# A de-interleaving turn of one input block laid out so that each phase is one copy, and a new seed for the order search

## The chip, the core and the metric

The kernel runs on one core of a Trainium2 chip. The metric is the device time of one execution in microseconds; the median of three runs of the kernel before is 252.25 us (252.25 to 252.41). Five engines work side by side: TensorE (PE, with its weight loads as PEld) multiplies, VectorE (DVE), ScalarE (ACT) and GpSimd (POOL) do elementwise work, and SyncE (SP) issues nearly all transfers.

## The reference

Two strided one-dimensional convolutions, a projection and a joint network. T is 4000, D is 512, both kernels have 5 taps, and U is 8.

```python
xp = jnp.pad(x, ((0,0),(pad,pad),(0,0)))
for i in range(K):
    h = h + jnp.einsum("btc,cd->btd", xp[:, i:i+T, :], w1[i])
h = _gelu(h)[:, ::2, :]
...
f = _gelu(f)[:, ::2, :]          # the same with w2 on h
fe = jnp.einsum("btd,de->bte", f, w_f)
ge = jnp.einsum("bud,de->bue", g, w_g)
j = jnp.tanh(fe[:, :, None, :] + ge[:, None, :, :])
return jnp.einsum("btud,dv->btuv", j, w_o)
```

Only even times of each convolution are kept. An output at time 2t needs inputs 2t-2 to 2t+2, so taps 0, 2 and 4 read only even input times (the even phase), and taps 1 and 3 only odd ones (the odd phase).

## The kernel before, in words

**Stages.** The first 426 outputs of the first convolution of batch 0 are computed directly, five taps each, while the rest of the inputs is still arriving (`direct`, line 811). The rest of both convolutions goes through fast products on triples of outputs (`Triple`, `Unit`), for which DVE and ACT form sums of input planes and of weights. Then come the projection (`fe`, `FeSeven`) and the joint network, in which ACT makes the tanh, DVE and POOL form sums and PE runs seven products per 4 tiles (`Seven`, `Plain`), with the results evicted by ACT and DVE and stored by SP.

**The direct stage.** Its input lies in `eo[phase, k, column]`: two phases, four channel groups k, channels on partitions. It is filled in two parts. Input block 0 (`xr[0]`, 512 times) is turned by PE transposes and copied by `turn(pp)` (line 610), one phase at a time. Input block 1 (`xr[1]`, 384 times, three consecutive times r = 0, 1, 2 on each of 128 partitions p, so that the time is 3p + r) is turned by `turn3` (line 628). It multiplies each 128x128 piece by `perm`, a permutation which puts the even partitions into the first 64 columns and the odd ones into the last 64. Since 3p + r is even when p and r have the same parity, one phase takes the even-partition half of r = 0 and r = 2 and the odd-partition half of r = 1. `turn3` before the change puts r = 0, 2, 1 into PSUM banks 4, 5, 6, each as (k, half, 64). ACT then copies out of them in four pieces: for each phase one piece with two of the three r (128x512) and one with the third (128x256). Each piece reads runs of 64 adjacent places and writes every third place of `eo`.

The order in which these steps are written down is: even turn of block 0, tap 0 on the 254 columns that block 0 covers, odd turn, tap 4 on them, `turn3`, tap 2 on them, then taps 0, 4, 2 on the remaining 172 columns (48 matmuls), and then taps 1 and 3 on all 426 columns (32 matmuls). Every tap is 4 output groups of 4 matmuls, accumulating in banks 0 to 3.

**What sets the order.** The program is a list of operations with the tiles that they read and write. `Plan.schedule` orders them per engine: `once` walks through a model of the engines with costs that are written down (for ACT 0.833 ns an element plus 0.05 us out of PSUM), taking on PE, SP and POOL the ready operation that was written first, on ACT and DVE the ready one with the earliest due time `late`. Evictions marked as flexible go to the engine that comes free. `learn` changes due times and puts holds on operations where the model has a gap on PE; `schedule` repeats that 600 times and keeps whatever does not make the modelled end later. The first six kinds of change are fixed ones, later ones are drawn from a random generator with the seed [4, tried]. Each engine then runs its list in order and waits on semaphores.

**Other names used below.** `w_sb` are the raw weights, `w_x` and `w_t` sums of weights made by DVE and ACT, `xa` and `xp` transposed input planes brought in by DMA transposes, `row` and `sd` intermediates of the triples; `acc` is PSUM. Line 507 is every matmul of `mm`, line 499 every ACT operation of `act`, line 494 every DVE operation of `tt`, line 654 the DVE multiply-add of `stt`, line 637 the matmul of `turn3`.

Of the kernel before, what the change touches and what calls it, by code (L numbers as in the profile page):

```python
# [7 lines left out]
ACT = mybir.ActivationFunctionType  # L8
ALU = mybir.AluOpType
BF16 = mybir.dt.bfloat16  # L10
FP16 = mybir.dt.float16
FP32 = mybir.dt.float32
P = 128
# [55 lines left out]
class Plan:  # L69
# [1 line left out]

    COMPUTE = ("pe", "act", "dve", "pool")
    HOP = 0.16
    PASSES = 600

    def __init__(self, nc):
        self.nc = nc
# [82 lines left out]
    def schedule(self, pred):  # L160
# [17 lines left out]
        best, tried = self.once(pred, succ, late, hold), 0  # L178
        for _ in range(self.PASSES):
            new = list(late), list(hold)  # L180
# [14 lines left out]
    def learn(self, pred, got, late, hold, tried):  # L195


        _, order, start, end, ready, _ = got
        place = {i: (e, p) for e, o in order.items() for p, i in enumerate(o)}
        gaps, t = [], 0.0  # L200
        for i in order["pe"]:
            if start[i] - t > 0.05 and start[i] > 6.0:
                gaps.append(i)
            t = end[i]
        if not gaps:
            return False
        kind, which = divmod(tried, len(gaps) + 1)
        if kind >= 6:
            rng = np.random.default_rng([4, tried])
            t = start[gaps[int(rng.integers(len(gaps)))]]  # L210
            for e in ("act", "dve"):
                for j in order[e]:
                    if t - 10.0 < start[j] < t and rng.random() < 0.15:
                        late[j] += float(rng.normal())
            return True
        step, wait = ((0.1, True), (0.5, False), (0.0, True), (2.0, True), (0.3, False), (1.0, True))[kind % 6]
        first = list(late)
        for i in gaps if which == len(gaps) else gaps[which:which + 1]:
            j = i
            for _ in range(30):  # L220
                done = [(end[q] + (self.HOP if w else 0.0), q) for q, w in pred[j].items()]
                if not done:
                    break
                q = max(done)[1]
                if self.ops[q].dma:
                    break
                e, p = place[q]
                if e in ("act", "dve") and p and start[q] > ready[q] + 0.03:
                    b = order[e][p - 1]
                    if wait and start[b] < ready[q] - 0.02 and first[b] > first[q]:  # L230
                        hold[b] = max(hold[b], ready[q] - 0.01)
                    late[q] -= step
                j = q
        return True
# [134 lines left out]
def bass_standalone__seq2seq_rnn_t_joint__speech_kernel(  # L369
# [22 lines left out]
    NK = D // P  # L392
# [12 lines left out]
    NT = 512  # L405
# [4 lines left out]
    with ExitStack() as es:  # L410
        cur = [16512]

        def at(name, shape, dtype, offset=None):
            o = cur[0] if offset is None else offset
            b = Buf(nc, name, shape, dtype, o)
            if offset is None:
                cur[0] = (b.end + 31) // 32 * 32
            return b
# [13 lines left out]
        xr = [Buf(nc, f"xr{i}", [4, NK, P], BF16, h_off + 16384 + i * 4096) for i in range(NX)]  # L432
# [7 lines left out]
        geT = at("geT", [NK * BU], FP32)  # L440
        gT = at("gT", [NK, BU], BF16)
        zero = at("zero", [NT], BF16)
        ident, perm = at("ident", [P], BF16), at("perm", [P], BF16)
        warm = at("warm", [2], FP32)
        xe = at("xe", [NK, 16], BF16)
        assert cur[0] <= 229368, cur[0]
        eo = Buf(nc, "eo", [2, NK, EW], BF16, w2_sb.end - w2_sb.bytes)
# [33 lines left out]
        ps = Psum(es.enter_context(nc.psum_tensor("acc", [P, 8 * NT], FP32)))  # L481
        block = es.enter_context(nc.Block(no_gpsimd_drain=True))
        pl = Plan(nc)
# [13 lines left out]
        def act(o, i, func, scale=1.0, bias=None):  # L497
            rd = (i,) if bias is None else (i, bias)
            pl.op("act", lambda e: e.activation(o.ap, i.ap, func, scale=scale,  # L499
                                                bias=0.0 if bias is None else bias.ap), rd, (o,),  # L500
                  o.ap.free_size() * 0.833e-3 + (0.05 if i.psum else 0.105 if bias is None else 0.186))

        def mm(o, pairs, start, stop, check=True):
# [13 lines left out]
        pl.op("pool", lambda e: e.affine_select(  # L517
            out=idv.ap, in_=zero[0:P].ap, compare_op=ALU.not_equal, fill=1.0, base=0,
            pattern=[[-1, P]], channel_multiplier=1), (zero[0:P],), (idv,))
        for i in range(2):  # L520
            pm = perm[i * P // 2:(i + 1) * P // 2]
            pl.op("pool", lambda e, pm=pm, i=i: e.affine_select(
                out=pm.ap, in_=zero[0:P // 2].ap, compare_op=ALU.not_equal, fill=1.0, base=-i,
                pattern=[[-2, P // 2]], channel_multiplier=1), (zero[0:P // 2],), (pm,))
        memset(eo[:, :, 15:16])
        memset(xa[:, :, 16 * -(-(NF + 2) // 16):16 * -(-(NF + 2) // 16) + 4])
# [5 lines left out]
        NR = (4, 3)  # L532
# [93 lines left out]
                    pl.op("dve", lambda e, o=o, v=v: e.tensor_copy(out=o.ap, in_=v.ap), (v,), (o,), vec_cost(o, (v,)))  # L626

        def turn3(cost):
            n, lo = NR[1], 16 + 2 * P
            place = [0, 2, 1]  # L630
            pv = [View(ps.h[:, (4 + i) * NT:(5 + i) * NT], np.array([4 + i]), True) for i in range(n)]
            for r in range(n):
                at_r = pv[place[r]]

                def fn(e, r=r, at_r=at_r):
                    for k in range(NK):
                        ins = e.matmul(at_r.ap[:, k * P:(k + 1) * P], lhsT=xr[1].h[:, r, k, :], rhs=perm.h[:, :],  # L637
                                       start=k == 0, stop=k == NK - 1, skip_group_check=True)
                    return ins
                pl.op("pe", fn, (xr[1][0:n], perm[:]), (at_r,), cost / n)  # L640

            def block(i0, i1, s0):
                ap = ps.h[:, (4 + i0) * NT:(4 + i1) * NT].rearrange("p (r k s c) -> p s k r c", r=i1 - i0, k=NK, s=2)
                return View(ap[:, s0], np.arange(4 + i0, 4 + i1), True)

            for pp in range(2):
                to = eo[pp, :, lo:lo + n * P // 2]
                for i0, i1, s0, o0 in ((0, 2, pp, pp), (2, 3, 1 - pp, 2 - 2 * pp)):
                    o = to.map(lambda a: a.rearrange("p k (c r) -> p k r c", r=n)[:, :, o0:o0 + i1 - i0, :])
                    act(o, block(i0, i1, s0), ACT.Copy)  # L650
                    pl.ops[-1].cost += 0.05

        def stt(eng, o, a, f, b):
            pl.op(eng, lambda e: e.scalar_tensor_tensor(  # L654
# [170 lines left out]
        turn(1, 0.43)  # L825
        direct(TAPS[1], 0, NH)
        turn3(0.67)
        direct(TAPS[2], 0, NH)
        for i in TAPS[:3]:
# [3 lines left out]
        for m in range(NK):  # L833
            v = ps.cols(m * NT, ND).map(lambda a: a.rearrange("p (q r) -> p r q", r=6))
# [447 lines left out]
        j = 2 + 4 * S1  # L1282
# [6 lines left out]
        fill = ["cc"] * 9 + ["c"] * 6 + ["p"] * 15  # L1289
# [4 lines left out]
        for i, q in enumerate(seven):  # L1294
            p = seven[i - 1] if i else None
            base = min([(p or q).jt] + plains[:1]) * P
            last = i + 1 == len(seven)
            r = []
# [60 lines left out]
```

## Time and profile before

| | |
|---|---|
| median of three runs | 252.25 us |
| the profiled execution | 252.33 us, its span 250.5 us |
| PE busy | 245.8 us (98%) |
| DVE, ACT busy | 210.1 us, 211.1 us (84% each) |
| POOL busy | 99.2 us (40%) |
| granted TensorE clock | 1.00 |

The time of an execution is the span of its instructions and some 1.8 us around it. Busy shares are averages: PE is the engine to look at, and what counts is where it stands still and who lets it go on.

### The profile page before, as it was taken

The page shows a single profiled execution, that of the slowest core. Times are in us where ns is not written, and L with a number is a line of the kernel's source. Part 1 is how long each engine was busy: PE and PEld are TensorE (multiplying, and loading weights), DVE is VectorE, ACT ScalarE, POOL GpSimd, SP SyncE. Part 2 cuts the span into 40 slices and gives each one's busy share as a digit, 9 for nine tenths or more (in the row PEclk, how much of TensorE's full clock was granted, in tenths as well). Part 3 has the DMA queues.
Part 4 walks back from the last instruction along what each step waited for, and adds up shares of the span by engine and source line. Part 5 has one row for each costly group of instructions (what it writes and reads, how often), then busy time and mean ns, then how long its engine had stood idle before and what let it go on. Part 6 is the DMA issues. An engine that isn't in the chain of part 4 may idle for free.

```text
span 250.5 us, 5277 instructions
## 1 busy us (share of the span) xinstructions
PE 245.8 (98%) x1948; PEld 183.3 (73%) x1948; DVE 210.1 (84%) x355; ACT 211.1 (84%) x351; POOL 99.2 (40%) x108
## 2 busy tenths in 40 slices
PE   8999999999999999999999999999999999999994
PEld 4777986666666666667556888777888878777883
DVE  2799998966999999398956889777999989986783
ACT  3399989859878767884599999999999999998772
POOL 2000000000000000000007978979799899888840
PEclk9999999999999999999999999999999999999999
DMA  6999999989000052000001043323345564555456
GB/s 224 322 213 188 168 187 168 188 162 352 7 3 0 0 166 89 0 4 0 0 3 42 0 147 109 125 86 111 120 152 167 167 190 154 165 177 183 150 191 207
DMA packets 54487, 31.86 MB, mean 127 GB/s; under 512 B 31518, under 2 KB 54206, under 8 KB 54462
## 3 DMA queue, kind: packets, MB, share of 16 engines
q1 hardware_dynamic: 54174, 31.37, 47.9%
q8 instruction: 15, 0.25, 0.4%
q10 hardware_dynamic: 288, 0.16, 0.2%
q14 instruction: 10, 0.08, 0.1%
HBM read 7.73 MB, written 16.38 MB: 96 GB/s over the span
## 4 chain that ended last, share of the span: by engine, by line
PE 97%; ACT 1%; ACTq 0%; issue 0%
PE acc L507 96%; ACT eo L499 1%; PE acc L618 1%; PE acc L637 0%; ACT og L1066 0%; ACTq L1092 0%; ACT ost L499 0%; ACTq L330 0%
## 5 line engine op out<-in xcount | busy, mean ns | idle before, releaser
L494 DVE TENSOR_TENSOR og<-acc,sn 128x512 bf16<-128x512 f32 x84 | 54.9, 682 | 7.9 <-PE acc L507 6.0
L499 ACT ACTIVATE jT<-feT,geT 128x1000 bf16<-128x1000 f32 (+5 forms) x60 | 57.5, 1017 | 0.3 <-DVE feT L494 0.3
L1146 POOL TENSOR_TENSOR ss<-jT 128x512 f16<-128x512 bf16 x33 | 38.5, 1175 | 41.3 <-DVE ss L1146 40.9
L507 PE MATMUL acc<-tw,ss 128*128 128x256 f16 x336 | 46.2, 273 | 0.0
L507 PE MATMUL acc<-row,w_sb 128*128 128x334 bf16 (+2 forms) x224 | 38.8, 296 | 0.0
L507 PEld LDWEIGHTS acc<-tw,ss 128*128 128x128 f16 x336 | 32.3, 98 | 7.6 <-ACT sn L1066 0.6
L507 PE MATMUL acc<-wo_sb,jT 128*128 128x256 bf16 (+1 forms) x208 | 33.3, 285 | 0.0
L1066 ACT ACTIVATE sn<-acc 128x512 f32<-128x512 f32 x48 | 29.7, 628 | 3.1 <-PE acc L507 2.3
L1067 DVE COPY sn<-acc 128x512 f32<-128x512 f32 x36 | 24.6, 685 | 7.0 <-PE acc L507 6.7
L507 PEld LDWEIGHTS acc<-row,w_sb 128*128 128x128 bf16 x224 | 21.1, 97 | 9.2 <-DVE acc L654 0.8
L491 POOL MEMSET hT<- 128x8 bf16 (+2 forms) x6 | 0.8, 148 | 61.8 <-ACT hT L499 45.0
L507 PEld LDWEIGHTS acc<-wo_sb,jT 128*128 128x128 bf16 x208 | 20.3, 98 | 5.0
L499 ACT ACTIVATE sd<-acc 128x334 f32<-128x334 f32 (+2 forms) x48 | 20.4, 432 | 3.4 <-PE acc L507 2.8
L1146 POOL TENSOR_TENSOR ss<-ss,jT 128x512 f16<-128x512 f16 x19 | 21.9, 1160 | 0.8 <-DVE ss L1146 0.8
L499 ACT ACTIVATE hT<-acc 128x334 bf16<-128x334 f32 (+3 forms) x36 | 15.5, 436 | 7.3 <-PE acc L507 6.7
L654 DVE SCALAR_TENSOR_TENSOR acc<-acc,sd 128x334 f32<-128x334 f32 (+2 forms) x24 | 11.6, 483 | 9.1 <-PE acc L507 9.0
L494 DVE TENSOR_TENSOR row<-row 128x1336 bf16<-128x1336 bf16 (+2 forms) x24 | 18.9, 796 | 0.0
L499 ACT ACTIVATE jX<-feT,geT 128x1000 bf16<-128x1000 f32 (+3 forms) x20 | 18.3, 963 | 0.0
L507 PE MATMUL acc<-xp,w_t 128*128 128x334 bf16 (+1 forms) x96 | 17.6, 305 | 0.0
L507 PE MATMUL acc<-hT,w_t 128*128 128x334 bf16 x96 | 17.5, 304 | 0.0
L507 PE MATMUL acc<-wo_sb,ss 128*128 128x256 bf16 x112 | 17.3, 273 | 0.0
L507 PE MATMUL acc<-xp,w_x 128*128 128x334 bf16 (+1 forms) x96 | 16.8, 305 | 0.0
(127 smaller groups left out, 496.7 us busy)
## 6 DMA issues: line engine op xcount, KB each, us to landing
out_dram<-og SPq DMA_DIRECT2D x42, 256.0 KB, 2.5
w_sb<-in_w_dram SPq DMA_DIRECT2D x10, 512.0 KB, 5.3
out_dram<-og SPq DMA_DIRECT2D x14, 128.0 KB, 2.1
out_dram<-ost SPq DMA_DIRECT2D x10, 128.0 KB, 1.9
xr<-in_x_dram SPq DMA_DIRECT2D x1, 512.0 KB, 3.4
wf_sb<-in_w_f_dram SPq DMA_DIRECT2D x1, 512.0 KB, 3.6
wg_sb<-in_w_g_dram SPq DMA_DIRECT2D x1, 512.0 KB, 4.7
wo_sb<-in_w_o_dram SPq DMA_DIRECT2D x1, 512.0 KB, 5.7
```

The source lines that it names most:

```text
L491: pl.op("pool", lambda e: e.memset(v.ap, 0.0), (), (v,))
L494: pl.op(eng, lambda e: e.tensor_tensor(out=o.ap, in0=a.ap, in1=b.ap, op=op), (a, b), (o,), 0.02 + 2.14e-3 * o.ap.free_size() if eng == "po ...
L499: pl.op("act", lambda e: e.activation(o.ap, i.ap, func, scale=scale, bias=0.0 if bias is None else bias.ap), rd, (o,), o.ap.free_size() * ...
L507: ins = e.matmul(o.ap, lhsT=l.ap, rhs=r.ap, start=start and n == 0, stop=stop and n == len(pairs) - 1, skip_group_check=not check)
L618: ins = e.transpose(pv.ap[:, r, k, :], xr[0].h[:, 2 * r + pp, 2 * h + k, :], ident.h[:, :])
L654: pl.op(eng, lambda e: e.scalar_tensor_tensor(out=o.ap, in0=a.ap, scalar=f, in1=b.ap, op0=ALU.mult, op1=add), (a, b), (o,), vec_cost(o, (a ...
L1066: pl.flex({"act": (lambda e: e.activation(o.ap, v.ap, ACT.Copy), 0.05 + n * 0.833e-3), "dve": (lambda e: e.tensor_copy(out=o.ap, in_=v.ap) ...
L1067: "dve": (lambda e: e.tensor_copy(out=o.ap, in_=v.ap), 0.065 + n * 1.04e-3)}, (v,), (o,))
L1146: fn = lambda e, o=S[i], x=x, y=y, op=op: e.tensor_tensor(out=o.ap, in0=x.ap, in1=y.ap, op=op)
```

## The change

Five edits. The permutation gets a third block of 64 columns that repeats the first, so that a slice of it also gives the order odd, even. `turn3` goes over k instead of r: for each k a bank holds six runs of 64 places, first the three of the even phase in the order of time, then the three of the odd phase; r = 1 writes the two middle runs together, r = 0 and r = 2 write one run in each half. It now uses banks 4 to 7. Each phase is then copied by one ACT operation over all four banks (128x768), even phase first; it reads every 64th place and writes adjacent places. The added 0.05 us in the planner's cost of these copies goes. The search takes 1200 rounds instead of 600, and another seed.

```diff
-    PASSES = 600
+    PASSES = 1200
...
-            rng = np.random.default_rng([4, tried])
+            rng = np.random.default_rng([13, tried])
...
-        ident, perm = at("ident", [P], BF16), at("perm", [P], BF16)
+        ident, perm = at("ident", [P], BF16), at("perm", [3 * P // 2], BF16)
...
-        for i in range(2):
+        for i in range(3):
             pm = perm[i * P // 2:(i + 1) * P // 2]
             pl.op("pool", lambda e, pm=pm, i=i: e.affine_select(
-                out=pm.ap, in_=zero[0:P // 2].ap, compare_op=ALU.not_equal, fill=1.0, base=-i,
+                out=pm.ap, in_=zero[0:P // 2].ap, compare_op=ALU.not_equal, fill=1.0, base=-(i % 2),
...
         def turn3(cost):
-            n, lo = NR[1], 16 + 2 * P
-            place = [0, 2, 1]
-            pv = [View(ps.h[:, (4 + i) * NT:(5 + i) * NT], np.array([4 + i]), True) for i in range(n)]
-            for r in range(n):
-                at_r = pv[place[r]]
-
-                def fn(e, r=r, at_r=at_r):
-                    for k in range(NK):
-                        ins = e.matmul(at_r.ap[:, k * P:(k + 1) * P], lhsT=xr[1].h[:, r, k, :], rhs=perm.h[:, :],
-                                       start=k == 0, stop=k == NK - 1, skip_group_check=True)
+            n, h, lo = NR[1], P // 2, 16 + 2 * P
+            for k in range(NK):
+                c0 = (4 + k) * NT
+                at_k = ps.cols(c0, 2 * n * h)
+
+                def fn(e, k=k, c0=c0):
+                    for r in range(n):
+                        if r % 2:
+                            o, pm = ps.h[:, c0 + 2 * h:c0 + 4 * h], perm.h[:, h:3 * h]
+                        else:
+                            o = ps.h[:, c0:c0 + NT].rearrange("p (s c) -> p s c", c=h)[:, r // 2:r // 2 + 5:4, :]
+                            pm = perm.h[:, 0:2 * h].rearrange("p (s c) -> p s c", s=2)
+                        ins = e.matmul(o, lhsT=xr[1].h[:, r, k, :], rhs=pm, start=r == 0, stop=r == n - 1,
+                                       skip_group_check=True)
                     return ins
...
             for pp in range(2):
-                to = eo[pp, :, lo:lo + n * P // 2]
-                for i0, i1, s0, o0 in ((0, 2, pp, pp), (2, 3, 1 - pp, 2 - 2 * pp)):
-                    o = to.map(lambda a: a.rearrange("p k (c r) -> p k r c", r=n)[:, :, o0:o0 + i1 - i0, :])
-                    act(o, block(i0, i1, s0), ACT.Copy)
-                    pl.ops[-1].cost += 0.05
+                v = ps.h[:, 4 * NT:8 * NT].rearrange("p (k j c) -> p k c j", k=NK, c=h)[:, :, :, n * pp:n * pp + n]
+                o = eo[pp, :, lo:lo + n * h].map(lambda a: a.rearrange("p k (c j) -> p k c j", j=n))
+                act(o, View(v, np.arange(4, 8), True), ACT.Copy)
```

More of the change, by code (lines that the diff above doesn't have):

```diff
@@ L628, in turn3 @@
         def turn3(cost):
-            n, lo = NR[1], 16 + 2 * P
-            place = [0, 2, 1]
-            pv = [View(ps.h[:, (4 + i) * NT:(5 + i) * NT], np.array([4 + i]), True) for i in range(n)]
-            for r in range(n):
-                at_r = pv[place[r]]
-                def fn(e, r=r, at_r=at_r):
-                    for k in range(NK):
-                        ins = e.matmul(at_r.ap[:, k * P:(k + 1) * P], lhsT=xr[1].h[:, r, k, :], rhs=perm.h[:, :],
-                                       start=k == 0, stop=k == NK - 1, skip_group_check=True)
-                    return ins
-                pl.op("pe", fn, (xr[1][0:n], perm[:]), (at_r,), cost / n)
@@ L642, in block @@
-            def block(i0, i1, s0):
-                ap = ps.h[:, (4 + i0) * NT:(4 + i1) * NT].rearrange("p (r k s c) -> p s k r c", r=i1 - i0, k=NK, s=2)
-                return View(ap[:, s0], np.arange(4 + i0, 4 + i1), True)
+            n, h, lo = NR[1], P // 2, 16 + 2 * P
[11 more added lines that the diff above has]
+                                       skip_group_check=True)
+                    return ins
+                pl.op("pe", fn, (xr[1][0:n], perm[:]), (at_k,), cost / NK)
```

## The prediction

> **What bounds the kernel now.** I read the page first, for the engine that is full:
>
> ```profile
> span 250.5 us, 5277 instructions
> PE 245.8 (98%) x1948; PEld 183.3 (73%) x1948; DVE 210.1 (84%) x355; ACT 211.1 (84%) x351; POOL 99.2 (40%) x108
> ```
>
> PE is busy for all but 4.7 us of 250.5. Then the chain of waits that ended last, in order of time, for what lies between PE's stretches:
>
> ```profile
> 5.89 3.84 PE acc L507 x32
> 9.73 0.68 PE acc L637 x12
> ...
> 10.44 2.33 ACT eo L499 x3
> ...
> 12.82 233.37 PE acc L507 x1852
> ```
>
> It leaves PE once before the end: after `turn3`'s matmuls (L637) it runs through three ACT copies into `eo`, 2.33 us, and then never leaves PE until 12.82 + 233.37 = 246.19. The waits of PE and of its weight loads, the second list after 12.9 us only, say the same:
>
> ```profile
> PE acc L507 <- PEq L1344: 0.8, 1, 0.8
> PE acc L507 <- ACT eo L499: 0.7, 1, 0.7
> ...
> PEld acc L507 <- DVE acc L654: 0.8, 3, 0.3
> PEld acc L507 <- ACT sn L1066: 0.6, 3, 0.3
> ...
> PEld acc L507 <- DVE xp L494: 0.2, 1, 0.2
> ```
>
> The matmuls have one wait inside the kernel, for `eo`. What the loads wait later (six such rows, from 0.8 down to 0.2, 2.6 us in all) is nearly all covered by matmuls still running, since PE shows no idle time of its own there. Now PE and ACT around the place, in order of time:
>
> ```profile
> 9.57 0.83 PE L637 MATMUL acc<-perm,xr 128*128 128x128 bf16 x12
> 10.24 1.90 PE L507 MATMUL acc<-eo,w_sb 128*128 128x254 bf16 x16
> 12.82 9.59 PE L507 MATMUL acc<-eo,w_sb 128*128 128x172 bf16 x80 [0.68 <-ACT eo L499]
> ```
> ```profile
> 5.24 1.26 ACT L499 ACTIVATE eo<-acc 128x512 bf16<-128x512 bf16 x2 [3.00 <-PE acc L618]
> ...
> 10.44 1.04 ACT L499 ACTIVATE eo<-acc 128x512 bf16<-128x512 f32 x1 [3.94 <-PE acc L637]
> 11.28 1.05 ACT L499 ACTIVATE eo<-acc 128x512 bf16<-128x512 f32 x1
> 12.14 1.05 ACT L499 ACTIVATE eo<-acc 128x256 bf16<-128x256 f32 x2
> 12.56 0.63 ACT L499 ACTIVATE eo<-acc 128x256 bf16<-128x256 f32 x1
> 12.99 0.84 ACT L499 ACTIVATE row<-xa 128x768 bf16<-128x768 bf16 x1
> 13.73 0.61 ACT L499 ACTIVATE w_x<-wu 128x512 bf16<-128x512 f32 x1
> ```
>
> The first two copies are the 512-wide pieces of the two phases and the last two their 256-wide rests. The even phase, which 48 matmuls need, is whole only with the third copy, which began at 12.14 and ended about 12.76 (0.63 long, as the fourth); PE goes on at 12.82.
>
> **The change part by part.**
>
> *The gate on PE.* The sixteen 254-wide matmuls take 1.90 us with the last one's own 0.27, so they follow each other every (1.90 - 0.27) / 15 = 0.109 us, and the next could have begun at 10.24 + 16 x 0.109 = 11.98. It began at 12.82: 0.84 us lost. The length of the new copy comes from these groups of ACT work:
>
> ```profile
> L499 ACT ACTIVATE eo<-acc 128x512 bf16<-128x512 f32 x2 | 1.9, 1044 | 3.9 <-PE acc L637 3.9
> L499 ACT ACTIVATE eo<-acc 128x512 bf16<-128x512 bf16 x2 | 1.2, 598 | 3.1 <-PE acc L618 3.0
> L499 ACT ACTIVATE feT<-acc 128x501 f32<-128x501 f32 x4 | 2.4, 603 | 0.0
> L1066 ACT ACTIVATE sn<-acc 128x512 f32<-128x512 f32 x48 | 29.7, 628 | 3.1 <-PE acc L507 2.3
> L499 ACT ACTIVATE row<-xa 128x768 bf16<-128x768 bf16 x3 | 2.5, 833 | 0.0
> ```
>
> Only the copies that write every third place are slow: 1044 ns against 628 for an eviction as wide. Copies that read PSUM in jumps and write adjacent places, as the new ones will (`turn`'s into `eo` 598, `feT` 603 for reads 167 places apart), are not slower. So 768 wide is between 0.83 (`row<-xa`) and, if the old pace holds (0.84 us from one 512-wide copy to the next, so 1.26 for 768, and 0.2 until the end), 1.46 us. I take 0.86, near `row<-xa` and a little up because the source is PSUM, and 0.76 until the next operation may begin. The even copy then ends at 10.44 + 0.86 = 11.30, before PE is through at 11.98. The whole 0.84 goes; what is late next there is nothing, with 0.6 us to spare. At the slow end it is whole at 11.90, and PE still does not wait. Were the odd copy put first, it would be ready at 10.44 + 0.76 + 0.86 + 0.06 = 12.12 and 0.14 would come back.
>
> *The matmuls of `turn3`.* Twelve stay twelve, 128 columns each, same weights; eight now write two runs of 64. Their 0.68 us in the chain stays if a jump in the output costs nothing (I take 0, since the columns streamed are the same); twice the pace for the eight would be 8 x 0.68 / 12 = 0.45 more, and with nothing in the rows that would make them faster the other end is 0. [...]
>
> *The third block of `perm`.* One more POOL operation of this kind:
>
> ```profile
> L522 POOL TENSOR_SCALAR_AFFINE_SELECT perm<-zero x2: 242/242/242, 1.6 to 1.8; 128x64 bf16<-128x64 bf16 x2
> ```
>
> 0.24 us at 2 us; the memsets queued behind it on POOL slip as much, the earliest reader of them (column 15 of `eo`) is PE at 5.89. It costs nothing, hidden by the wait for the first input; bare it would cost 0.24. Bank 7, newly used, is free: the odd turn's copy out of it was the second of two that ended at 5.24 + 1.26 = 6.50, and the triples take that bank only behind the 80 matmuls that end at 12.82 + 9.59 = 22.41; cost 0. No DMA and nothing on SP's queue is moved.
>
> *What follows PE.* An earlier PE must be fed earlier. ACT is free at 10.44 + 2 x 0.76 = 11.96 instead of 12.99, 1.03 sooner. Its next input has landed by then: the first transpose into `xa` was issued at 5.59 and took 5.4 us.
>
> ```profile
> 5.59 3.14 SPq L549 DMA_TRANSPOSE xa<-in_x_dram  x2
> ...
> DMA to landing us min/median/max: 5.4/5.4/5.4
> ```
>
> DVE has less to gain, as its timeline and the table of stretches show (PE, PEld, DVE, ACT, POOL busy):
>
> ```profile
> 12.05 0.68 DVE L494 TENSOR_TENSOR ssum<-ws,w_sb 128x512 f32<-128x512 f32 x1
> 12.66 0.68 DVE L494 TENSOR_TENSOR w_t<-ws,w_sb 128x512 bf16<-128x512 f32 x1
> 13.86 0.56 DVE L494 TENSOR_TENSOR row<-row,xa 128x768 bf16<-128x768 bf16 x1 [0.52 <-ACT row L499]
> ...
> 26.77 0.35 DVE L654 SCALAR_TENSOR_TENSOR acc<-acc,sd 128x190 f32<-128x190 f32 x1
> ```
> ```profile
> 12.80:26.00 13.20, 13.18 (x126) 10.40 (x127) 12.66 (x27) 13.09 (x27) 0.36 (x3) 1.00 1.15 201
> 26.00:38.00 12.00, 12.00 (x128) 10.64 (x126) 12.00 (x23) 11.25 (x22) 0.42 (x3) 1.00 1.12 169
> ```
>
> Its only idle time between 12.8 and 38 is the one before 13.86, waiting for ACT's `row`. DVE operations of this kind follow each other every 0.61 us (12.05 to 12.66), so it could go on at 13.27; with `row` ready at 11.96 + 0.84 + 0.06 = 12.86 it will. DVE comes 0.59 us earlier, and after that it is full. PE takes DVE's results just in time in this stretch: the multiply-add of 26.77 ends at 27.12 and PE's next matmul, which needs it, starts at 27.21:
>
> ```profile
> 27.21 0.33 PE L507 MATMUL acc<-row,w_sb 128*128 128x190 bf16 x2
> ```
>
> With the usual 0.06 from one engine's end to the next one's start that leaves 0.03 of slack, so in this order PE keeps 0.59 + 0.03 = 0.62 of the 0.84. An order that brings the multiply-add forward, before weight sums that nobody needs yet, would keep up to 0.84; I take 0.65. After 38 us PE is full and a shift of all passes through to the end.
>
> *The order search.* The new seed and the new costs reorder ACT and DVE wherever they had a choice. Bounded from the rows: all later waits gone would give at most the 2.6 us above, and really far less, since PE itself shows none; downwards one long operation in a bad place costs up to its own length (rival A). I take 0.
>
> **Sum**, against the profiled execution: 252.33 - 0.65 = 251.68, which is 251.6 against the median, 0.08 below it.
>
> **The rivals.**
>
> *A, slower: a new just-in-time wait from the order.* DVE holds operations of over 2 us, and one stands right before a multiply-add that releases PE:
>
> ```profile
> 77.75 2.25 DVE L494 TENSOR_TENSOR row<-row,hT 128x4032 bf16<-128x4032 bf16 x1
> 79.92 0.50 DVE L654 SCALAR_TENSOR_TENSOR acc<-acc,sd 128x334 f32<-128x334 f32 x1
> ...
> 80.48 0.74 PE L507 MATMUL acc<-row,w_sb 128*128 128x334 bf16 x4
> ```
>
> PE's group of 80.48 starts 0.06 after the end of that multiply-add: the wait is already used up. If the new order lets such an operation start 1.5 us later against PE, PE stands for it: -0.65 + 1.5 = +0.85, so 253.1. It decides from 1.2 us upward (0.65 gained and 0.5 to be seen). For it: two engines are 84% full and the search models times. Against: the model's order of before left PE without such a wait in 233 us. Chance 0.17.
>
> *B, no change: the copies stay slow.* If it is not the writing at every third place that costs, the two copies take 2 x 1.26 and ACT is free at 12.96 as before; DVE gets nothing, and PE runs into it at 27.21 with only 0.03 kept, at most 0.2 by a better order: about 252.1. Rows against it are those at 598 and 603. [...] With B belongs an order that gives back about half of the 0.65. Together 0.21.
>
> *C, the change does less than it says:* `turn3`'s matmuls slow down by 0.45: the gain is 0.65 - 0.45 = 0.2, 252.05. Chance 0.04, within no change.
>
> **How the numbers follow.** This kernel's measurement tells about 0.2% (0.5 us) from no change. The forecast (gain 0.5 to 1.0) has 0.58, B and C 0.25, A 0.17; so faster 0.58, same 0.25, slower 0.17. The likeliest alone reaches from 251.2 (0.84 kept and 0.2 of the later waits gone) to 251.75. For 8 in 10 the range must take B and C and the smaller part of A: 251.1 to 252.7; beyond it lie most of A and a better order than I see.
>
> **What would show it.** In the profile after: two ACT copies 128x768 of about 0.86 us, the even one ended by 11.3; no idle time of PE before the 172-wide matmuls, which start near 11.98; twelve L637 matmuls of 219 ns at the old pace (0.68 us in all); DVE without its gap at 13.3; the PE chain ending about 0.65 earlier than 246.19, so near 245.5. I am wrong if the copies take 1.4 us (B), if L637 takes over 1 us (C), or if a new wait of PE over 0.5 us stands after 13 us (A).

## The result, and the profile after

The changed kernel took 251.97 us in the median of its first series (251.48 to 252.64), where the kernel before took 252.26 (252.17 to 252.69): a ratio of 0.998, with a 95% interval of 0.9972 to 0.9988. Two later series, each beside new runs of the kernel before, gave 0.9972 (0.9962 to 0.9983) and 0.9965 (0.9952 to 0.9977). By the ratios it is faster by 0.5, 0.7 and 0.9 us, by the medians by 0.3, 0.6 and 1.1; the forecast gain of 0.65 lies within both. The first median, 251.97, is 0.4 above the forecast 251.6 and above the likeliest stretch (251.2 to 251.75), but inside the stated range. The profiled execution took 251.69, 0.64 less than that of before.

The page first:

```profile
span 249.9 us, 5278 instructions
PE 245.9 (98%) x1948; PEld 183.7 (74%) x1948; DVE 209.9 (84%) x355; ACT 210.1 (84%) x349; POOL 99.4 (40%) x109
```

Busy times hardly moved; only ACT has 1.0 us less, since two copies replace four slow ones. What moved is the chain that ended last, in order of time:

```profile
6.05 3.71 PE acc L507 x32
9.76 0.67 PE acc L641 x12
10.43 235.12 PE acc L507 x1868
245.55 0.02 issue
```

Before, it left PE for three ACT copies of 2.33 us and returned at 12.82. Now it stays on PE from `turn3`'s matmuls (now L641) to the end at 245.55, 0.64 sooner than 246.19. The twelve matmuls take 0.67 us where they took 0.68. ACT's timeline around the copies (first the stretch, then the first copy alone):

```profile
10.47 1.51 ACT L499 ACTIVATE eo<-acc 128x768 bf16<-128x768 f32 x2 [3.79 <-PE acc L641]
11.87 0.63 ACT L499 ACTIVATE w_x<-wu 128x512 bf16<-128x512 f32 x1
...
10.47 0.81 ACT L499 ACTIVATE eo<-acc 128x768 bf16<-128x768 f32 x1 [3.79 <-PE acc L641]
```

The even copy is 0.81 us long and over at 11.28; the 172-wide matmuls, no longer set apart from the 254-wide ones in the timeline, begin at 12.00 without a wait. (Their start is called the gate from here on: PE passes it when the even phase of `eo` is whole.) ACT is free at 11.87 instead of 12.99. DVE no longer stands still before `row`:

```profile
12.54 0.68 DVE L494 TENSOR_TENSOR w_t<-ws,w_sb 128x512 bf16<-128x512 f32 x1
13.15 0.68 DVE L651 SCALAR_TENSOR_TENSOR wu<-w_sb 128x512 f32<-128x512 bf16 x1
13.75 0.56 DVE L494 TENSOR_TENSOR row<-row,xa 128x768 bf16<-128x768 bf16 x1
```

The weight loads wait a little behind the gate, in other places than before:

```profile
PEld acc L507 <- DVE acc L651: 0.2, 1, 0.2
PEld acc L507 <- ACT sd L499: 0.2, 1, 0.2
PEld acc L507 <- issue: 0.2, 1, 0.2
```

These are all loads' waits from 12.9 to 60 us. Two of them reach the matmuls: PE's steps at 23.84 (behind `sd`) and 28.25 ("issue") are 0.12 and 0.13 us too long.

Most of what follows compares three starts on PE, read off its timeline in narrow windows: that of tap 4, whose weights are the second load; that of the 172-wide matmuls (the gate); and that of the last matmul. The last column holds all that PE loses behind the gate, to be compared with the 234.23 of before (differences are taken before rounding).

| kernel | tap 4 | gate | last matmul | gate to last |
|---|---|---|---|---|
| before | 7.81 | 12.82 | 247.05 | 234.23 |
| after, three profiles | 7.86, 7.66, 7.99 | 12.00, 11.81, 12.15 | 246.41, 246.23, 246.57 | 234.41, 234.42, 234.42 |
| layout, order of before, two profiles | 7.85, 8.01 | 12.01, 12.17 | 246.74, 246.43 | 234.73, 234.26 |
| even phase first, old layout | 7.75 | 12.09 | 247.31 | 235.22 |
| new search, old layout | 7.75 | 12.76 | 247.52 | 234.76 |
| old search, new layout | 7.83 | 11.98 | 246.67 | 234.69 |
| late third load, old layout | 8.00 | 13.02 | 247.22 | 234.21 |
| late third load, new layout | 7.71 | 12.14 | 246.44 | 234.31 |
| sums on POOL | 7.98 | 12.14 | 248.14 | 236.00 |
| two DVE operations less | 8.27 | 12.43 | 246.67 | 234.24 |

### The profile page after: what moved, and what is told of

The parts are those of the page before. It is cut to its first block, busy times and chain, and to the rows that moved or that the text cites. A ratio compares the mean times of both kernels' runs of the same rounds, so it can differ in the third digit from the quotient of the medians.

```text
span 249.9 us, 5278 instructions
## 1 busy us (share of the span) xinstructions
PE 245.9 (98%) x1948; PEld 183.7 (74%) x1948; DVE 209.9 (84%) x355; ACT 210.1 (84%) x349; POOL 99.4 (40%) x109
## 4 chain that ended last, share of the span: by engine, by line
PE 98%; ACT 0%; ACTq 0%; issue 0%
PE acc L507 97%; PE acc L618 1%; PE acc L641 0%; ACT og L1063 0%; ACTq L1089 0%; ACT ost L499 0%; ACTq L330 0%
```

## The experiments

### The layout alone

Except for the unaltered repeats and the two kernels under "The search alone", the kernels of these experiments are ordered by hand: in place of the model and the search they return the engine lists that the kernel before runs by, and only the stated operations differ.

```diff
     def schedule(self, pred):
-        ops, HOP, n = self.ops, self.HOP, len(self.ops)
...
-        return order
+        order, self.start = json.loads(zlib.decompress(base64.b64decode(ORDER)))
...
+        return order
```

> The new layout of the second turn alone: every engine runs the list of before, except that the two wide copies stand where the four pieces stood, and the third piece of the permutation is made. My theory (the layout does all of it, and DVE's supply caps what PE keeps): PE has no idle time ahead of the 172-wide matmuls, DVE loses its 0.5 us gap, a small new wait of PE of some 0.2 us appears near 26.5 us for the multiply-add, and PE's last stretch ends 0.55 to 0.7 us before the 246.2 of before: ratio about 0.9975. Rival (the search brings the gain): PE ends within 0.2 us of before. Rival (all of the 0.84 is kept): PE ends 0.8 us sooner, without a new wait.

Measured: 251.63 us in the median against 252.34, ratio 0.9972 (0.9963 to 0.9982). The layout does the whole of the gain, with no help from the search. Its profile was taken in its longest execution (252.03), in which PE's last matmul starts only 0.31 us sooner than before, not the 0.55 to 0.7 expected. It shows where PE can give back what the gate gained, DVE first, then PE:

```profile
17.28 0.56 DVE L494 TENSOR_TENSOR row<-row,xa 128x768 bf16<-128x768 bf16 x1
18.16 0.43 DVE L494 TENSOR_TENSOR w_t<-w_sb 128x512 bf16<-128x512 bf16 x1 [0.33 <-DMA w_sb<-in_w_dram]
...
25.58 0.36 DVE L651 SCALAR_TENSOR_TENSOR acc<-acc,sd 128x190 f32<-128x190 f32 x1
```
```profile
25.41 0.49 PE L507 MATMUL acc<-xa,w_x 128*128 128x190 bf16 x4
26.00 0.50 PE L507 MATMUL acc<-row,w_sb 128*128 128x190 bf16 x4
26.33 0.49 PE L507 MATMUL acc<-xa,w_t 128*128 128x190 bf16 x4
26.86 0.83 PE L507 MATMUL acc<-row,w_sb 128*128 128x190 bf16 x8
```

Here a weight load landed late and DVE lost 0.33 us at 17.8; the chain that ended last runs from this landing through DVE to PE's 26.00. DVE was full up to the multiply-add that ends at 25.94, and PE's group of 26.00 started right behind it; four matmuls follow each other in 0.33 us in this stretch, so 26.00 is 0.26 and 26.86 is 0.20 late. That is the stretch that the prediction had named, with 0.46 instead of 0.2 us, since the late landing comes on top.

> The layout with the order of before once more, unaltered, beside the changed kernel on one chip. My theory: ratio to before 0.997 to 0.9975. Against the changed kernel the two theories are: the new order costs 0.2 to 0.3 us (its two series so far gave 0.998 and 0.9972), or the two are the same within 0.1 us.

Measured beside the changed kernel on one chip: 251.69 us, ratio 0.9967 (0.9955 to 0.998). In this profile no wait at 26 us is left and only 0.03 us more than before is lost behind the gate. That is not because DVE keeps up with the whole 0.84: the second weight load landed late, so the gate opened only 0.65 us sooner than before, and DVE's multiply-add comes as much sooner:

```profile
26.12 0.36 DVE L651 SCALAR_TENSOR_TENSOR acc<-acc,sd 128x190 f32<-128x190 f32 x1
```

Before, this operation started at 26.77.

> The changed kernel once more, unaltered, for a second profile and on the same chip as the others. My theory (its profile of 0.64 us under that of before was one of its better executions, and the new order costs it 0.2 to 0.3 us against the layout with the order of before): median 251.8 to 252.0 where before has 252.3, new waits of PE between 20 and 30 us as in its first profile (0.12 and 0.13 us at 23.8 and 28.3). Rival (the first profile was typical): median 251.6 to 251.7.

Measured: 251.82 us where before had 252.46, ratio 0.9972 (0.9962 to 0.9983). By the median it was the first theory, by the ratio nearer to the second, since the kernel before had a higher median here too. Ratios are what can be compared between series, and this one does not show that the new order costs anything.

> The changed kernel a third time, on the chip of the two others. The new order costs something: ratio 0.9978 to 0.9983 of before where the layout with the order of before has 0.997 to 0.9975. It costs nothing: the same ratio as that one within 0.0005.

Measured: 251.54 us, ratio 0.9965 (0.9952 to 0.9977), against 0.9967 of the layout with the order of before on the same chip. The new order costs nothing that can be measured in time. In the profiles it loses some 0.16 us more behind the gate (234.42 against 234.26 in the second profile of the layout), less than a series can tell.

### The gate without the supply

The order of ACT's list in words:

```diff
 ACT's list:
-  eo(even, two r), eo(odd, two r), eo(even, third r), eo(odd, third r)
+  eo(even, two r), eo(even, third r), eo(odd, two r), eo(odd, third r)
```

> The old layout with its four slow copies and the order of before, only that ACT takes both pieces of the even phase before those of the odd one. That opens PE's gate sooner but frees ACT no sooner: the second piece of a phase shares words of eo with the first and waits until it has ended. Rival (what counts is the gate on PE alone): the even phase is whole near 12.15, PE goes on at 12.2 instead of 12.8 and the kernel is 0.6 us faster, nearly what the change gave. My theory (ACT and DVE must come sooner too): PE starts the 172-wide matmuls 0.6 us sooner, ACT is free 0.4 us later (near 13.45 instead of 12.99), DVE's gap grows from 0.5 to about 0.9 us, PE gives the 0.6 back in new waits between 22 and 31 us, and the kernel is not faster: 0 to 0.5 us slower.

Measured: 252.6 us, ratio 1.0015 (1.0006 to 1.0023): slower. PE's gate opened 0.73 us sooner (12.09), and all of it and more was lost again, most of it in one wait. PE's timeline, then ACT's, then DVE's:

```profile
21.52 1.15 PE L507 MATMUL acc<-xa,w_x 128*128 128x190 bf16 x12
23.37 0.50 PE L507 MATMUL acc<-row,w_x 128*128 128x190 bf16 x4 [0.70 <-ACT sd L499]
```
```profile
10.37 3.17 ACT L499 ACTIVATE eo<-acc 128x512 bf16<-128x512 f32 x4 [3.83 <-PE acc L637]
13.33 0.84 ACT L499 ACTIVATE row<-xa 128x768 bf16<-128x768 bf16 x1
...
22.26 0.84 ACT L499 ACTIVATE xa<-xa 128x760 bf16<-128x760 bf16 x1
22.99 0.54 ACT L499 ACTIVATE sd<-acc 128x190 f32<-128x190 f32 x2
```
```profile
12.37 0.69 DVE L494 TENSOR_TENSOR w_t<-ws,w_sb 128x512 bf16<-128x512 f32 x1
14.20 0.57 DVE L494 TENSOR_TENSOR row<-row,xa 128x768 bf16<-128x768 bf16 x1 [1.14 <-ACT row L499]
```

The four copies took 2.96 us until the next operation started (13.33 - 10.37) instead of 2.55 (12.99 - 10.44), DVE's gap grew from 0.52 to 1.14, and at 23.37 PE waited for `sd`, which ACT reached only at 22.99 behind its backlog. It was ACT that came late there, where I had looked at DVE. ACT started `row` 0.34 us later than before, and of that 0.11 was left at `sd` (22.99 against 22.88). Without this 0.11 PE's group would have started at 23.26, just where it started before; that is worked out from these rows, no run has it. So a gate that opens sooner gains nothing while ACT's work ends when it did: that ACT is free 1.1 us sooner is as much a part of this change as the gate.

### The search alone

```diff
-    PASSES = 600
+    PASSES = 1200
...
-            rng = np.random.default_rng([4, tried])
+            rng = np.random.default_rng([13, tried])
```

> The old layout with the new seed and 1200 rounds. My theory (the search decides nothing large): the 0.68 us wait ahead of the 172-wide matmuls stays, the waits behind it change by 0.2 us at most, ratio 0.999 to 1.001. Rival (the search brings a part of the gain): PE ends at least 0.3 us before 246.2.

Measured: 252.79 us, ratio 1.0023 (1.0012 to 1.0033). Neither theory: the search alone makes the old layout slower by some 0.5 us. The wait for `eo` stayed, and behind the gate PE lost 0.53 us more than before. PE's waits (the second is that for the first weight load, ahead of the gate), and its timeline where it loses most of it:

```profile
PE acc L507 <- ACT eo L499: 0.7, 1, 0.7
PE acc L507 <- DMA w_sb<-in_w_dram: 0.6, 1, 0.6
```
```profile
35.13 0.49 PE L507 MATMUL acc<-xa,w_t 128*128 128x190 bf16 x4
35.64 1.87 PE L507 MATMUL acc<-row,w_x 128*128 128x336 bf16 x12
...
40.87 0.74 PE L507 MATMUL acc<-xp,w_x 128*128 128x336 bf16 x4
41.65 0.74 PE L507 MATMUL acc<-row,w_sb 128*128 128x336 bf16 x4
```

Between 30 and 42 us PE's steps are some 0.6 us too long in sum, the longest at 35.64 (0.18) and 41.65 (0.21). The second stands right behind a DVE multiply-add that ended at 41.59; for the first the profile names no releaser.

```diff
-    PASSES = 1200
+    PASSES = 600
...
-            rng = np.random.default_rng([13, tried])
+            rng = np.random.default_rng([4, tried])
```

> The new layout with the search as before (600 rounds, the old seed), which orders ACT and DVE anew for it. My theory: the same as the changed kernel within 0.2 us, PE without a gap ahead of the 172-wide matmuls, ending near 245.5. Rival (the new seed matters): it gives back over 0.3 us in waits behind 13 us, or is over 0.2 us faster than the changed kernel.

Measured: 251.84 us, ratio 0.9987 (0.9977 to 0.9996), against 0.9972 of the layout with the order of before on the same chip. The two intervals overlap a little, so the time speaks for the rival without deciding it. In the profile PE lost 0.46 us more behind the gate than in the kernel before, over the rival's 0.3, and 0.28 more than in the changed kernel. So in PE's profile either layout loses 0.3 to 0.5 us with the search that was not its own. The edit changes the number of rounds together with the seed, so these two runs speak of the order that was drawn and not of the seed alone. They suggest that the changed kernel needed its new search, not to gain anything but to lose nothing; the two were not run in one series.

### The cushion that the change used up

```diff
+        dummy = row[1][5].map(lambda a: a.rearrange("p k c -> p (k c)")[:, 0:NT])
+        pl.dma("sp", lambda e: e.dma_start(dummy.ap, x[0, 0:P, :]), (), (dummy,), nbytes=P * 1024)
         came.append(load_w1(TAPS[2], came[0]))
```

> The kernel before with its own order, and one more transfer of 128 KB (into a buffer not yet in use) issued right ahead of the third weight load, that of tap 2, so that this load and all behind it land some 0.4 us later. My theory (before the change, PE's wait ahead of the 172-wide matmuls and DVE's gap at 13.3 us are a cushion behind this landing): PE starts tap 2 about 0.4 us later, waits only 0.3 to 0.5 us for the copies instead of 0.7 to 0.85, and the end moves by 0.1 us or less. Rival (there is no cushion): slower than before by the delay of the landing, 0.3 to 0.5 us.

Measured: 252.53 us, ratio 1.0005 (0.9996 to 1.0014). PE's timeline shows the delay being swallowed:

```profile
9.76 0.83 PE L639 MATMUL acc<-perm,xr 128*128 128x128 bf16 x12
10.88 1.91 PE L507 MATMUL acc<-eo,w_sb 128*128 128x254 bf16 x16 [0.28 <-DMA w_sb<-in_w_dram]
13.02 1.15 PE L507 MATMUL acc<-eo,w_sb 128*128 128x172 bf16 x13 [0.23 <-ACT eo L499]
```

Tap 2 started 0.45 us behind its place, and the wait for the copies shrank from 0.68 to 0.23: from the start of tap 4 to the gate it is 5.02 us, as in the kernel before (5.01).

> The new layout with the order of before, and the same extra transfer ahead of the load of tap 2. My theory (the layout has used up the cushion): the delay reaches the end, 0.3 to 0.5 us slower than the same kernel without it (ratio 0.9972), so about 0.9985 to 0.999 of before; PE stands at tap 2 until the weights land and has no wait for the copies. Rival (cushion or not makes no difference): the same 0.1 us or less as in the kernel before, ratio near 0.9975.

Measured: 252.16 us, ratio 0.9992 (0.9983 to 1.0), against 0.9972 and 0.9967 without the transfer: 0.5 to 0.6 us slower, where the kernel before lost 0.1. The intervals of the two kernels' losses are wide, but the direction is that of the cushion. The profile, of the fastest execution (251.73), shows the delay on PE:

```profile
9.45 0.83 PE L643 MATMUL acc<-perm,xr 128*128 128x128 bf16 x12
10.39 3.79 PE L507 MATMUL acc<-eo,w_sb 128*128 128x254 bf16 x41
```

Tap 2 could have begun at 9.45 + 0.67 = 10.12 and waited 0.27 us for its weights; no wait for the copies follows, and from tap 4 to the gate it is 4.43 us instead of 4.16. In the new layout a late landing of the third load, that of tap 2, reaches the end.

### More room on DVE

```diff
-                tt("dve", w1_t[2, :, sl], t, w(2), add)
+                tt("pool" if m else "dve", w1_t[2, :, sl], t, w(2), add)
```

> The new layout with the order of before, and three weight sums of 0.68 us each (w_t out of wv and w_sb, for the second, third and fourth group) moved from DVE to POOL, which stands idle there. My theory (DVE's supply caps what PE keeps): DVE reaches the multiply-adds near 26 and 27 us 0.6 to 1.2 us sooner, PE's waits there (0.26 and 0.20 us in the layout with the order of before) go, and the kernel ends 0.2 to 0.4 us before that one: ratio 0.996 to 0.9965. Rival (the cap is elsewhere, ACT or the landings): the waits stay or come back within a few us, ratio 0.997 or more. Rival (POOL's work lengthens DVE's operations beside it): DVE's 0.68 us operations take over 0.8 us there, and nothing is gained.

Measured: 253.32 us, ratio 1.0037 (1.0024 to 1.0049). The third theory, and worse than it said. POOL's and DVE's timelines:

```profile
10.54 1.56 POOL L494 TENSOR_TENSOR w_t<-ws,w_sb 128x512 bf16<-128x512 f32 x1 [7.99 <-DVE ws L494]
```
```profile
11.00 1.65 DVE L494 TENSOR_TENSOR ssum<-ws,w_sb 128x512 f32<-128x512 f32 x1
12.58 0.68 DVE L651 SCALAR_TENSOR_TENSOR wu<-w_sb,wu 128x512 f32<-128x512 bf16 x1
13.18 0.68 DVE L494 TENSOR_TENSOR ssum<-ws,w_sb 128x512 f32<-128x512 f32 x1
```

DVE's sum that began beside POOL's operation took 1.65 us instead of 0.68. Each of the three moved operations saved DVE 0.6 us and cost it about 1.0. PE paid through ACT: ACT waited 0.70 us for one of DVE's weight sums, and PE then waited 0.71 for ACT's `sd` at 23.43. DVE's sum took 0.97 us longer and ended 0.55 us after POOL's operation of 10.54; by what it was held up the run does not show.

```diff
-                stt("dve", u, w(2), 2.0, u)
+                m < 2 and stt("dve", u, w(2), 2.0, u)
```

> The new layout with the order of before, and two of DVE's multiply-adds (wu out of w_sb and wu, third and fourth group of output channels, 0.60 us each from one start to the next) left out near 16 us, so that the term of tap 2 is missing from one weight sum of half the channels; nothing else moves. My theory (DVE's supply is what keeps PE from the whole 0.84 us): DVE is 1.2 us sooner at the multiply-adds near 26 us, PE's waits there go, and it ends some 0.2 us before the layout with the order of before. Rival (ACT or the landings cap it just as well): the waits stay, or others of the same size take their place, and the time is that of the layout with the order of before within 0.1 us.

Measured: 251.66 us, ratio 0.996 (0.9947 to 0.9974), where the layout with the order of before had 251.69 and 0.9967 on the same chip. The medians differ by 0.03 us, the ratios by 0.0007 where each interval reaches 0.0013 to either side, so the time does not tell a gain of 0.2 from none. Nor did the edit give DVE the room that it was to give. DVE's timeline shows two new waits:

```profile
17.23 0.56 DVE L494 TENSOR_TENSOR row<-row,xa 128x768 bf16<-128x768 bf16 x1 [0.72 <-ACT row L499]
22.63 0.56 DVE L494 TENSOR_TENSOR xa<-xa 128x760 bf16<-128x760 bf16 x1 [0.29 <-ACT xa L499]
```

Of the 1.2 us that were left out, 1.0 went into waiting for ACT. The multiply-add that started at 26.77 before starts at 26.37, 0.40 us sooner. The gate opened only 0.39 us sooner, because the second weight load landed late, and PE kept 0.38 of it. So in this execution ACT held DVE as soon as DVE had room. The run does not say what PE would keep of 0.84 with a faster DVE; that stays open.

## Why the prediction was right

**The gate (0.84 us).** Right in place and size: PE has no idle time there, and starts at 12.00 where 11.98 was forecast. From the start of tap 4 to the gate it was 5.01 us and is 4.14 to 4.16.

**The copies.** 0.81 us instead of 0.86, and 0.70 instead of 0.76 until the next start. The row with strided reads and adjacent writes (`feT`, 603 ns for 501 elements) was the one to go by; rival B is not what happened. The copies fell from about 1.64 ns an element (0.84 us from one start to the next for 512) to 0.92 (0.707 for 768) when the writes became adjacent. The reads changed with the writes, from runs of 64 to single places 64 apart, and no run has the one without the other; that jumping reads did not make the copies slow is the ground for laying it to the writes.

**The matmuls of `turn3`.** Taken at 0, measured -0.01. Rival C did not happen: the twelve took 0.67 us where they took 0.68, though eight of them now wrote two runs of 64. No run shows the doubled time of these eight, from which its 0.45 us came.

**What follows PE.** The need for supply was right: in `even_first` an earlier gate without an earlier ACT gained nothing. DVE's gap closed as forecast, and the term "PE keeps 0.59 + 0.03 = 0.62" holds where the order is that of before. The three profiles of the new layout in that order, each against the kernel before (us sooner):

| profile | gate | DVE's multiply-add of 26.77 | last matmul |
|---|---|---|---|
| layout, first (a late landing at 18.16) | 0.81 | 0.32 | 0.31 |
| layout, second | 0.65 | 0.65 | 0.62 |
| layout with the late third load | 0.68 | 0.61 | 0.61 |

To 0.03 us PE keeps what DVE gains. In the first and the third, PE's group starts right behind that multiply-add (26.45 + 0.35 and 26.86; 26.16 + 0.36 and 26.58); in the second the gate had gained no more than DVE, so nothing was lost at that place. In the changed kernel the search had moved these operations. There PE lost 0.18 or 0.19 us in all three profiles, the size that the sum had, but at other places: in the first profile at 23.84, behind ACT's `sd`, and at 28.25, where the profile names no releaser. That this size came out in an order that the sum had not looked at is luck.

**The order search.** "I take 0" came out for this pair of layout and search, on one chip 0.9965 against 0.9967. But the step's reasoning was too light. I had bounded the search by the waits of before and by one long operation in a bad place; `search_only` and `layout_old_search` show that an order drawn by the other search loses 0.3 to 0.5 us on PE without any such operation. Rival A is real, in a smaller size, spread over several waits. That it did not happen here the prediction had not worked out; it was luck.

**What is late next.** "Nothing, with 0.6 us to spare" holds for the place that it speaks of. In all eight profiles of the new layout without the extra transfer the gate comes 4.14 to 4.16 us behind the start of tap 4, and PE's own work from there is 16 x 0.109 + 0.67 + 16 x 0.109 = 4.16. When tap 4 itself is late, so is the gate. In four profiles PE waits there for the second weight load, as in the changed kernel's third:

```profile
7.99 0.61 PE L507 MATMUL acc<-eo,w_sb 128*128 128x254 bf16 x4 [0.33 <-DMA w_sb<-in_w_dram]
```

The others are the second of the layout (0.32), the one with two DVE operations less (0.55) and, with the old layout, `late_before` (0.17). This is nothing new: before the change too the gate came 5.01 or 5.02 us behind tap 4, late or not, since `turn3` and its copies stand behind tap 4, and the wait for the copies hid none of it. What that wait did hide is a late third load, and this the prediction left out: with it the old layout still has 5.02 us, and the new one 0.27 more than its 4.16.

## What to carry to other kernels

Before you take away a wait, ask two things: which engines must come sooner for the gain to last, and which landing was hidden by the wait. In the three profiles of the new layout in the order of before, the gain that lasted was, to 0.03 us, the smallest of what the engines in turn gained: 0.62 and 0.61 us where DVE gained 0.65 and 0.61, 0.31 where a late landing left DVE 0.32, and not the 0.84 of the wait. When a copy is slow, look whether it writes or reads in jumps; here moving the jump from the SBUF write to the PSUM read nearly halved its time per element (1.64 to 0.92 ns), at no cost to the matmuls that lay the data out (0.68 and 0.67 us). With an order found by a random search, hold the order fixed to measure an edit, because the redrawn order alone moved this kernel nearly as much as the edit did (ratio 1.0023 against 0.9965 to 0.998). And compare a profile by differences inside it, from one start to a later one, since a late landing ahead of both shifts the whole profile: in the changed kernel's third profile PE waited 0.33 us for one at tap 4, and from the gate to the last matmul it still took 234.42 us, as in the second.

## What the runs showed of the hardware

An ACT copy that writes every third bf16 place took 1044 ns for 512 elements; one that reads every 64th fp32 place of PSUM and writes adjacent places took 811 ns for 768. Twelve matmuls of 128 columns took 0.67 us when eight of them wrote two runs of 64 places with a jump between, and 0.68 when all wrote without a jump. A DVE sum of two SBUF operands went from 0.68 to 1.65 us beside a POOL operation of the same kind. The second weight load landed between 5.7 and 6.6 us after its issue in the thirteen profiles, and where it was late PE stood up to 0.55 us for it (0.17 in the one profile of the old layout that shows this wait).
